# u's products over four token tiles at a time, with their operand kept in the places of two sequence tiles

## The chip, the cores and the metric

The kernel runs on one core of one Trainium2 chip. The metric is device time in microseconds (us), the median of several executions.

## What is computed

The reference mixes two branches with a gate, over S = 2048 tokens of D = 640 features:

```python
g = sigmoid((x * gate_w).sum(-1))             # one gate for each token
a = Cr @ (x @ dre.T) - Ci @ (x @ dim.T)       # Fourier mixing: sequence matrices 2048x2048, hidden 640x640
q = x @ w_q                                   # 32 heads, two halves of 128
s1, s2 = q1 @ k1.T, q2 @ k2.T                 # 16 scores a half; the best two of each, then the best two pairs
act = gelu(x @ u[e].T);  b = sum(g_e * act * v[e])   # 256 experts, two for each head
out = g * a + (1 - g) * b
```

## The kernel before, in words

Everything is float32 at full precision on TensorE: each operand is split into a high and a low part (ScalarE rounds the high part, VectorE or GpSimd subtracts to get the low one), and each product is three matmuls, high by high, high by low, low by high (`mm3`, lines 141 to 145).

**The sequence stage** is the backbone. `seq_piece(n)` (line 229) runs for n = 0 to 127. Piece n multiplies one 128x512 block of a sequence matrix (a "piece", tile `WS`, loaded as `wf`) by one split tile X[s] of x (s = n % 16, 128 tokens by 640 features, high and low): 15 matmuls of 512 columns into banks 0 to 4. Sixteen pieces make a round, with one round for each 512 columns of each of the two sequence matrices. Each piece loads piece n+5 and splits piece n+3.

**Where X lies.** Sixteen split tiles do not fit in SBUF beside the rest. In the first round (pieces 0 to 15) all sixteen lie in places X0 to X15. Tiles 0 to 8 (`AWAY = 9`) are stored to DRAM once (`put_x`, line 449, into `xd`), and their places serve others from then on. In later rounds they come back through places X6, X7 and X8 in turn (`get_x`, line 452, three pieces ahead of use). From about piece 64 they return for good.

**What is hung on the pieces.** After each piece, `follow(n)` (line 202) issues what `at(n, ...)` has put there, in the order in which it was put, so the program order of every engine and of every DMA queue is fixed when the kernel is built. Nearly all loads go through one queue, that of SyncE (SP). Each engine and the SP queue do their instructions in order, and an instruction that waits holds those behind it.

**Stage 1 (pieces 0 to 29)** also folds the query weights with the keys. The 32 loads of `wq` (640 KB each, five buffers, `load_wq` at line 353) are multiplied four at a time in `w_part` (line 358) after pieces 6, 9, ..., 27. VectorE transposes the results, and `split_w` and `make_t` prepare the score weights WU and tw. `load_u` and `split_u` bring u^T in after pieces 21 to 27. The first `store_piece` (five stores from ScalarE's queue) comes after piece 24.

**Stage 2 (pieces 30 to about 66)** computes the scores. Tokens go in eight pairs p of 128-token tiles. `split_xT(p, n)` splits x^T of a pair into `xh` and `xl` (places of their own), `sum_xT` and `split_sums_xT` make the sums for a Strassen-Winograd scheme, and `score_step(p, a)` with a = 0 to 3 runs after four pieces in a row; a piece without a step follows each odd pair. Step 0 runs six matmuls into bank 5, then `u_pair(p)` (line 720): for both halves of the experts, 15 matmuls of 256 columns into bank 7, one Gelu on ScalarE, two stores to `actd`. Then bank 5 is copied into bank 7 as the start of the next products.

**Stage 3 (pieces 66 to 127)** adds the experts' sums, built on VectorE and multiplied in groups of 48 small matmuls (line 815). **The last stage** (70 steps) applies the hidden matrices and v.

Of the kernel before, what the change touches and what calls it, by code (L numbers as in the profile page):

```python
# [17 lines left out]
P = 128  # L18
S = 2048
D = 640  # L20
# [3 lines left out]
WARM = 19  # L24
# [3 lines left out]
TC = 512  # L28
NC = S // TC
NPC = 2 * NC * NT  # L30
KD = D // P
# [7 lines left out]
KZ = KD + 1  # L39
NSTEP = 7 * KZ  # L40
AHEAD = 5
AWAY = 9
BYPASS = 4
ACCUM_END = NT * (NC + 2) - 4

# [61 lines left out]
def gated_mix_kernel(ctx: ExitStack, tc: tile.TileContext, xT, xn, dreT, dimT, wsre, wsim, wq, kT, uT, vv, gw, out):  # L107
    nc = tc.nc
# [3 lines left out]
    big = ctx.enter_context(tc.tile_pool(name="big", bufs=1))  # L112
# [9 lines left out]
    def bank(n, shape=(P, TC), dt=F32):  # L122
        return psum.tile(list(shape), dt, name=f"b{n}", tag=f"b{n}")
# [4 lines left out]
    def ps_t(shape, dt=F32):  # L128
        return bank(7, shape, dt)
# [6 lines left out]
    def split(f, h, l, eng):  # L136

        nc.scalar.activation(h, f, AF.Copy)  # L138
        eng.tensor_sub(l, f, h.bitcast(F32))  # L139

    def mm3(o, wh, wl, ah, al, first, last, more=False):

        nc.tensor.matmul(o, wh, ah, start=first, stop=False, skip_group_check=more)  # L143
        nc.tensor.matmul(o, wh, al, start=False, stop=False, skip_group_check=more)  # L144
        nc.tensor.matmul(o, wl, ah, start=False, stop=last, skip_group_check=more)  # L145
# [3 lines left out]
    actd = dram.tile([2, P, S], F32, name="actd")  # L149
# [5 lines left out]
    def run_bg(us):  # L155
        bg.run(us, share)
# [39 lines left out]
    def at(n, f, *args):  # L196
        then.setdefault(n, []).append(lambda: f(*args))
# [63 lines left out]
    p1 = p1_stack.enter_context(tc.tile_pool(name="p1", bufs=1, reuse_waits="tile"))  # L261
    pools = [p1]

    def load_x(s):
        if s < NT:
            if s % 2 == 0:
                xr[s // 2] = big.tile([P, 2, D], F32, name="xr", tag=("xf", "xh", "xl")[s // 2 % 3])
            nc.sync.dma_start(xr[s // 2][:, s % 2], xn[s])

    def split_x(s):  # L270

        if s < NT:
            X[s] = big.tile([P, 2, D], F32R, name="X", tag=f"X{s}")
# [32 lines left out]


    warm = nc.const_aps.tensor(1.0, [P, 2 * P], mybir.dt.bfloat16)
    t = ps_t([P, 2 * P])
    for n in range(WARM):  # L310
        nc.tensor.matmul(t, warm[:, :P], warm, start=True, stop=True)  # L311

    split_x(0)
    load_piece(4)
# [105 lines left out]
    def split_xT(p, n):  # L420

        if p < NP:
            if not xs:
                xs.update((t, big.tile([P, 2, KD, P], F32R, name=t, tag=t)) for t in ("xh", "xl"))
            split(xf[p][:, n], xs["xh"][:, n], xs["xl"][:, n], nc.gpsimd)

    SX = {}

# [21 lines left out]
        nc.sync.dma_start(xd[s], X[s].bitcast(F32))  # L450

    def get_x(s, tag):
        X[s] = big.tile([P, 2, D], F32R, name="X", tag=f"X{tag}")
# [76 lines left out]
    def x_part(n, k0, k1):  # L530
        return [[xs[t][:, n, k] for k in range(k0, k1)] for t in ("xh", "xl")]
# [12 lines left out]
    def score_step(p, a):  # L544


        i0, i1 = 2 * p, 2 * p + 1
        copy = lambda o, f: nc.scalar.activation(o, f, AF.Copy)  # L548
        if a == 0:
            AB["A"] = bank(5)  # L550
            products(AB["A"], (x_part(0, 0, 2), w_part2(0, 2, 0)), first=True)
            split_sums_xT(p)
            u_pair(p)
            AB["Z"] = bank(7)
            copy(AB["Z"], AB["A"])
        elif a == 1:
            products(AB["Z"], (x_part(0, 2, 4), w_part2(2, 4, 0)), (x_part(0, 4, 5), w_part2(4, 5, 0)))
            new_sc(i0)
            copy(sc_half(i0, 0), AB["Z"])
            AB["Y"] = bank(6)  # L560
            products(AB["Y"], (s_part(1), t_part(1)), first=True)
            AB["Z"] = bank(7)
            copy(AB["Z"], AB["Y"])
            load_xT(p + 1)
        elif a == 2:
            products(AB["A"], (s_part(2), t_part(2)))
            copy(sc_half(i0, 1), AB["A"])
            products(AB["Z"], (s_part(4), w_part2(2, 4, 1)), (x_part(0, 4, 5), w_part2(4, 5, 1)))
            nc.vector.tensor_add(sc_half(i0, 1), sc_half(i0, 1), AB["Z"])
            bg.credit -= 0.75  # L570
            picks(i0, scs.pop(i0))
            products(AB["A"], (s_part(3), t_part(3)))
            new_sc(i1)
            copy(sc_half(i1, 1), AB["A"])
            split_xT(p + 1, 0)
        else:
            products(AB["Y"], (x_part(1, 4, 5), w_part2(4, 5, 1)))
            nc.vector.tensor_add(sc_half(i1, 1), sc_half(i1, 1), AB["Y"])
            products(AB["A"], (x_part(1, 2, 4), t_part(4)), (x_part(1, 4, 5), w_part2(4, 5, 0)))
# [137 lines left out]
        if i % NB == NB - 1:  # L717
            bg.add(gates(i // NB))

    def u_pair(p):  # L720
        xh, xl = xs["xh"], xs["xl"]
        ps = bank(7, (P, 2, 2 * P))
        for n in range(2):
            c = slice(n * P, (n + 1) * P)
            for k in range(KD):
                mm3(ps[:, n, :], UH[:, k, c], UL[:, k, c], xh[:, :, k, :], xl[:, :, k, :], k == 0 and n == 0, k == KD - 1, True)
            run_bg(1.8)
        act = p2.tile([P, 2, 2 * P], F32, name="act")
        nc.scalar.activation(act, ps, AF.Gelu_apprx_tanh)
# [184 lines left out]
    def split_sums(k):  # L914
        if k == KD:
            f = p3.tile([P, 4 * TC], F32R, name="ts", tag="hot0")
            TS[8] = f[:, :2 * D]
            raw_free.append(f[:, 2 * D:2 * D + TC].bitcast(F32))
            raw_tags.extend((("xf", 2), ("X9", 2)))
        for n in () if k == KD else [k] + ([5 + k // 2] if k % 2 == 0 else []):  # L920
            TS[n] = big.tile([P, 2 * D], F32R, name="ts", tag=f"X{(1, 3, 4, 5, 6, 0, 2, 7)[n]}")
        t = T["t"]
        t1, t5, t3, t6 = (t[:, n * 2 * P:(n + 1) * 2 * P] for n in range(4))
        for n, f in enumerate((t1, t3, t5, t6, t[:, 8 * P:])):
            split(f, t_sum(k, n, 0), t_sum(k, n, 1), nc.gpsimd if n < 2 else nc.vector)
        bg.credit -= 1.0

    def load_v():
        T[KD] = big.tile([P, 2, D], F32, name="dt", tag="X9")
        nc.sync.dma_start(T[KD], vv.rearrange("k p d -> p k d"))  # L930

    def split_v():
# [13 lines left out]
    at(NPC + 14, store_gates, 1)  # L946


    fresh, raw_free = deque(), deque()
    raw_tags = [("X8", 2)] + [("wf", 1)] * 4 + [("X10", 2), ("wf", 1)] + [(f"X{s}", 2) for s in range(11, 16)]  # L950
    raw, sp = {}, {}

    def take(key):
# [305 lines left out]
```

## Time and profile before

| | |
|---|---|
| median of 3 runs | 754.41 us (753.17 to 755.41) |
| the profiled execution | 753.44 us, span from first to last instruction 751.7 us |
| TensorE (PE) | busy 746.7 us, 99% of the span |
| VectorE (DVE), ScalarE (ACT), GpSimd (POOL) | busy 587.4, 361.7 and 346.6 us |
| DMA | 165.89 MB, mean 221 GB/s |
| score stage in the trace | pieces 31 to 65, about 132 to 378 us |

In the profile, PE are the matmuls and PEld the weight loads, which overlap. A matmul's end is modelled and the matmuls are pipelined, so the distance between two starts, not the duration of one, is what a matmul costs in a row of them. SPq and ACTq are the DMA queues of SyncE and ScalarE. A row of the timeline shows start, time and line of an instruction (or of several alike, merged), and in brackets how long its engine stood idle before it and what ended that. "To landing" is the time from the issue of a DMA to the arrival of its last byte.

### The profile page before, as it was taken

Reading aid. Unit: us, or ns where it says so; the run is one execution under the profiler, and the core shown is the slowest. Engines: PE = TensorE matmul, PEld = TensorE weight load, DVE = VectorE, ACT = ScalarE, POOL = GpSimd, SP = SyncE. Lnnn points to the kernel's source line nnn. Section 1 sums busy time; section 2 is a strip of 40 time slices with the busy share of each in tenths; the row PEclk is TensorE's granted clock in tenths of the full one; section 3 lists DMA queues with packets and bytes.
Section 4 is the critical chain, followed back from the end, with each engine's and each line's share of the span. In section 5 each row is a group of like instructions: output and inputs, shape, how many; then the busy total and the mean of one; then the engine's idle time right before and its main releaser. Section 6 shows DMA issues by size and latency. Waiting matters only on the chain.

```text
span 751.7 us, 11366 instructions
## 1 busy us (share of the span) xinstructions
PE 746.7 (99%) x4045; PEld 610.7 (81%) x4045; DVE 587.4 (78%) x741; ACT 361.7 (48%) x660; POOL 346.6 (46%) x286
## 2 busy tenths in 40 slices
PE   9999999999999999999999999999999999999998
PEld 7777777888888888888888888888888888888887
DVE  6864088278999999998999888979999983357651
ACT  4334134534345835553734687633555653443451
POOL 5533225342424424334345445643356793487253
PEclk9999999999999999999999999999999999999999
DMA  9999999478366786663496856388766689775301
GB/s 334 378 388 356 342 381 345 132 191 278 57 174 149 184 273 164 159 167 118 121 376 210 175 146 203 116 255 291 264 225 209 218 261 335 228 233 182 112 29 71
DMA packets 84490, 165.89 MB, mean 221 GB/s; under 512 B 16081, under 2 KB 23377, under 8 KB 84177
## 3 DMA queue, kind: packets, MB, share of 16 engines
q1 hardware_dynamic: 70960, 140.89, 55.5%
q0 software_dynamic: 5472, 9.96, 8.6%
q10 hardware_dynamic: 8000, 14.31, 5.2%
q8 instruction: 32, 0.52, 0.3%
q14 instruction: 26, 0.20, 0.1%
HBM read 132.46 MB, written 31.08 MB: 218 GB/s over the span
## 4 chain that ended last, share of the span: by engine, by line
PE 96%; DMA 2%; DVE 2%; issue 0%; SPq 0%; ACT 0%
PE b L143 30%; PE b L144 30%; PE b L145 30%; PE b L239 2%; PE b L365 2%; DMA wq<-in_wq 2%; PE b L815 1%; PE b L311 1%; DVE ST L217 1%; DVE WU L139 0%; DVE tw L139 0%; DVE wp L371 0%; ACT WU L138 0%; DVE tt L397 0%; DVE tt L396 0%
## 5 line engine op out<-in xcount | busy, mean ns | idle before, releaser
L143 PE MATMUL b<-WS,X 128*128 128x512 f32 x620 | 243.5, 393 | 0.0
L144 PE MATMUL b<-WS,X 128*128 128x512 f32 x620 | 241.5, 389 | 0.0
L145 PE MATMUL b<-WS,X 128*128 128x512 f32 x620 | 241.3, 389 | 0.0
L139 POOL TENSOR_TENSOR WS<-wf,WS 128x512 fp32r<-128x512 f32 x89 | 135.9, 1532 | 162.8 <-ACT WS L138 157.9
L143 PEld LDWEIGHTS b<-WS,X 128*128 128x128 f32 x620 | 116.4, 188 | 28.0 <-issue 4.1
L145 PEld LDWEIGHTS b<-WS,X 128*128 128x128 f32 x620 | 116.4, 188 | 24.5
L144 PEld LDWEIGHTS b<-WS,X 128*128 128x128 f32 x620 | 116.4, 188 | 23.3
L138 ACT ACTIVATE WS<-wf 128x512 fp32r<-128x512 f32 x89 | 55.7, 629 | 76.9 <-PE b L145 32.1
L803 DVE TENSOR_TENSOR hot<-rows,wtab 128x1024 f16<-128x1024 f16 x64 | 62.7, 1005 | 0.7 <-PE b L815 0.6
L139 POOL TENSOR_TENSOR WS<-ra,WS 128x512 fp32r<-128x512 f32 x39 | 55.1, 1426 | 15.3 <-ACT WS L138 13.2
L139 POOL TENSOR_TENSOR xl<-xf,xh 128x640 fp32r<-128x640 f32 x16 | 28.2, 1767 | 69.3 <-ACT xh L138 62.9
L138 ACT ACTIVATE WS<-ra 128x512 fp32r<-128x512 f32 x55 | 34.5, 631 | 50.9 <-PE b L145 36.0
L548 ACT ACTIVATE sc<-b 128x512 f32<-128x512 f32 x32 | 19.2, 600 | 80.7 <-PE b L145 80.7
L191 POOL DMA_DIRECT2D WS<-in_wsre x30 | 26.4, 880 | 68.0 <-ACT WS L189 66.6
L773 ACT ACTIVATE b<-b,mask 128x128 f32<-128x128 f32 x128 | 43.0, 342 | 13.5 <-PE b L815 10.4
L139 POOL TENSOR_TENSOR WP<-ra,WP 128x512 fp32r<-128x512 f32 x18 | 26.4, 1482 | 43.2 <-ACT WP L138 43.1
L598 DVE TENSOR_TENSOR eq<-sc,mm 128x1024 f16<-128x1024 f32 x32 | 41.4, 1293 | 0.9
L605 DVE TENSOR_REDUCE tied<-eq 128x64 f32<-128x1024 f16 x32 | 39.0, 1219 | 0.9
L596 DVE TENSOR_REDUCE mm<-sc 128x64 f32<-128x1024 f32 x32 | 38.8, 1212 | 0.3
L217 DVE SCALAR_TENSOR_TENSOR ST<-ST,grow 128x512 f32<-128x512 f32 x40 | 31.4, 846 | 0.6 <-ACT ST L246 0.6
L143 PE MATMUL b<-WU,xh 128*128 128x512 f32 x80 | 31.2, 391 | 0.0
L145 PE MATMUL b<-WU,xl 128*128 128x512 f32 x80 | 31.1, 389 | 0.0
(203 smaller groups left out, 1468.8 us busy)
## 6 DMA issues: line engine op xcount, KB each, us to landing
wq<-in_wq SPq DMA_DIRECT2D x32, 640.0 KB, 7.1
X<-xd SPq DMA_DIRECT2D x30, 640.0 KB, 6.6
wf<-in_wsim SPq DMA_DIRECT2D x64, 256.0 KB, 4.8
wf<-in_wsre SPq DMA_DIRECT2D x63, 256.0 KB, 6.5
ra<-pd SPq DMA_DIRECT2D x47, 256.0 KB, 3.7
pd<-ST ACTq DMA_DIRECT2D x35, 256.0 KB, 5.2
WS<-in_wsre POOLq DMA_DIRECT2D x30, 256.0 KB, 5.3
xd<-X SPq DMA_DIRECT2D x9, 640.0 KB, 9.4
```

The lines of the kernel that those rows point to most:

```text
L138: nc.scalar.activation(h, f, AF.Copy)
L139: eng.tensor_sub(l, f, h.bitcast(F32))
L143: nc.tensor.matmul(o, wh, ah, start=first, stop=False, skip_group_check=more)
L144: nc.tensor.matmul(o, wh, al, start=False, stop=False, skip_group_check=more)
L145: nc.tensor.matmul(o, wl, ah, start=False, stop=last, skip_group_check=more)
L191: nc.gpsimd.dma_start(l, (wsre, wsim)[w][c, s], accum_op=OP.add)
L217: nc.vector.scalar_tensor_tensor(f, f, -1.0 if w else 1.0, g, op0=OP.mult, op1=OP.mult)
L596: nc.vector.tensor_reduce(m, sc, op=OP.max, axis=AX.X)
L598: nc.vector.tensor_tensor(eq, sc, m[:, :, None].to_broadcast([P, HH, E]), op=OP.is_equal)
L605: nc.vector.tensor_reduce(tied[:, s, ib, :], eq, op=OP.add, axis=AX.X)
L773: nc.scalar.activation(f[:, :, n], f[:, :, n], AF.Copy, scale=mask4[:, n:n + 1])
L803: nc.vector.tensor_tensor(o, a, b, op=op)
```

## The change

`u_pair(p)`, once for each of the eight pairs with 256 columns, becomes `u_pairs(c)`, once for two pairs with 512 columns, in step 0 of the odd pairs. For that, split x^T of two pairs must lie in SBUF together: `xh` and `xl` double to four tiles (5 KB more a partition each). They take the places of sequence tiles: X9 and X10 become one double place that holds `xh`, X11 and X12 another that holds `xl`. The places freed (the old ones of `xh` and `xl`) hold X[11] and X[12] during the score stage. ScalarE copies them there after pieces 16 and 17 and back after piece 66 (`move_x`). X[9] and X[10] are held in DRAM instead (`AWAY = 11`): they are stored after pieces 19 and 21, come back through places X6 and X7 in the second and third rounds, and are loaded for good after pieces 70 and 71. The first two loads of the hidden matrices (`load_dd`) move from pieces 70 and 72 to 71 and 74, and the buffers of the last stage are taken from the double places in another way.

The core of the diff:

```diff
-AWAY = 9
+AWAY = 11
+    def place(tag):
+        if tag in (9, 11):
+            TWIN[tag] = big.tile([P, 2, 2, D], F32R, name="X", tag=f"X{tag}")
+        if tag in (9, 10, 11, 12):
+            return TWIN[tag - (tag + 1) % 2][:, (tag + 1) % 2]
+        return big.tile([P, 2, D], F32R, name="X", tag=f"X{tag}" if isinstance(tag, int) else tag)
+
+    def move_x(s, tag):
+        old, X[s] = X[s], place(tag)
+        nc.scalar.activation(X[s], old.bitcast(F32), AF.Copy)
...
-                xs.update((t, big.tile([P, 2, KD, P], F32R, name=t, tag=t)) for t in ("xh", "xl"))
-            split(xf[p][:, n], xs["xh"][:, n], xs["xl"][:, n], nc.gpsimd)
+                xs.update((t, big.tile([P, 2, 2, KD, P], F32R, name=t, tag=tag)) for t, tag in (("xh", "X9"), ("xl", "X11")))
+            split(xf[p][:, n], xs["xh"][:, p % 2, n], xs["xl"][:, p % 2, n], nc.gpsimd)
...
-        at(6 + 2 * s, put_x, s)
+        at(6 + 2 * s if s < 9 else 1 + 2 * s, put_x, s)
     for s in range(3):
         at(2 * NT - 5 + s, get_x, s, 6 + s)
+    for s, tag in ((11, "xh"), (12, "xl")):
+        at(s + 5, move_x, s, tag)
...
             split_sums_xT(p)
-            u_pair(p)
+            act = u_pairs(p // 2) if p % 2 else lambda: None
             AB["Z"] = bank(7)
             copy(AB["Z"], AB["A"])
+            act()
...
-    def u_pair(p):
+    def u_pairs(c):
         xh, xl = xs["xh"], xs["xl"]
-        ps = bank(7, (P, 2, 2 * P))
+        def act(n, ps):
+            f = p2.tile([P, TC], F32, name="act")
+            nc.scalar.activation(f, ps, AF.Gelu_apprx_tanh)
+            nc.sync.dma_start(actd[n][:, c * TC:(c + 1) * TC], f)
         for n in range(2):
-            c = slice(n * P, (n + 1) * P)
+            e = slice(n * P, (n + 1) * P)
+            ps = bank(7 - n)
             for k in range(KD):
-                mm3(ps[:, n, :], UH[:, k, c], UL[:, k, c], xh[:, :, k, :], xl[:, :, k, :], k == 0 and n == 0, k == KD - 1, True)
-            run_bg(1.8)
-        act = p2.tile([P, 2, 2 * P], F32, name="act")
-        nc.scalar.activation(act, ps, AF.Gelu_apprx_tanh)
-        for n in range(2):
-            nc.sync.dma_start(actd[n][:, 2 * p * P:2 * (p + 1) * P], act[:, n])
+                mm3(ps, UH[:, k, e], UL[:, k, e], xh[:, :, :, k, :], xl[:, :, :, k, :], k == 0, k == KD - 1)
+                run_bg(0.68)
+            if n == 0:
+                act(n, ps)
+        return lambda: act(1, ps)
...
+    for s in (11, 12):
+        at(N1, move_x, s, s)
...
-        at(N1 + 4 + 2 * m, load_dd, m)
+        at(N1 + 5 + 3 * m, load_dd, m)
```

Where the change moves instructions, the program order shows it. On the SP queue, from the load of piece 23 on (after piece 18), before; `wq` are the query weights, `wf` sequence pieces, `xd<-X` a store of a sequence tile, `xf` the x^T of the first pair:

```order
L356 DMA wq<-in_wq 128x1280 x2
L177 DMA wf<-in_wsre 128x512
L356 DMA wq<-in_wq 128x1280 x2
L177 DMA wf<-in_wsre 128x512
L450 DMA xd<-X 128x1280
L177 DMA wf<-in_wsre 128x512
L356 DMA wq<-in_wq 128x1280 x2
L418 DMA xf<-in_xT 128x640 x2
```

and the same place with the change:

```order
L371 DMA wq<-in_wq 128x1280 x2
L177 DMA wf<-in_wsre 128x512
L465 DMA xd<-X 128x1280
L371 DMA wq<-in_wq 128x1280 x2
L177 DMA wf<-in_wsre 128x512
L465 DMA xd<-X 128x1280
L177 DMA wf<-in_wsre 128x512
L465 DMA xd<-X 128x1280
L371 DMA wq<-in_wq 128x1280 x2
L433 DMA xf<-in_xT 128x640 x2
```

The store of X[9] (640 KB) now stands ahead of the last nine loads of `wq` in this queue, and that of X[10] ahead of the last seven. On ScalarE, step 0 of the first pair before (`b_1279` is bank 5, `b_1294` and `b_1329` are bank 7):

```order
L138 ACTIVATE tw<-xf 128x256 x2
L138 ACTIVATE h<-xf 128x256 x2
L729 ACT_TABLE_LOAD
L729 ACTIVATE act<-b_1294 128x512
L548 ACTIVATE b_1329<-b_1279 128x512
```

and step 0 of the second pair with the change (`b_1479` is bank 5, `b_1495` and `b_1537` bank 7, `b_1518` bank 6):

```order
L138 ACTIVATE tw<-xf 128x256 x2
L138 ACTIVATE h<-xf 128x256 x2
L745 ACT_TABLE_LOAD
L745 ACTIVATE act<-b_1495 128x512
L565 ACTIVATE b_1537<-b_1479 128x512
L745 ACTIVATE act<-b_1518 128x512
```

An odd pair now has two Gelus around the copy, and an even pair has none: its copy follows the four splits at once.

More of the change, by code (lines that the diff above doesn't have):

```diff
@@ L262, in gated_mix_kernel @@
     pools = [p1]
+    TWIN = {}
+    def place(tag):
[7 more added lines that the diff above has]
+        nc.scalar.activation(X[s], old.bitcast(F32), AF.Copy)
     def load_x(s):
@@ L272, in split_x @@
         if s < NT:
-            X[s] = big.tile([P, 2, D], F32R, name="X", tag=f"X{s}")
+            X[s] = place(s)
             f = xr[s // 2][:, s % 2]
@@ L308, in gated_mix_kernel @@
     warm = nc.const_aps.tensor(1.0, [P, 2 * P], mybir.dt.bfloat16)
-    t = ps_t([P, 2 * P])
+    t = ps_t([P, TC])
     for n in range(WARM):
-        nc.tensor.matmul(t, warm[:, :P], warm, start=True, stop=True)
+        c = slice(0, 2 * P) if n < WARM - 1 else slice(2 * P, TC)
+        nc.tensor.matmul(t[:, c], warm[:, :P], warm, start=n < WARM - 1, stop=True, skip_group_check=n == WARM - 1)
     split_x(0)
@@ L528, in products, with x_part @@
             run_bg(0.68)
-    def x_part(n, k0, k1):
-        return [[xs[t][:, n, k] for k in range(k0, k1)] for t in ("xh", "xl")]
+    def x_part(p, n, k0, k1):
+        return [[xs[t][:, p % 2, n, k] for k in range(k0, k1)] for t in ("xh", "xl")]
     def s_part(n):
@@ L550, in score_step @@
             AB["A"] = bank(5)
-            products(AB["A"], (x_part(0, 0, 2), w_part2(0, 2, 0)), first=True)
+            products(AB["A"], (x_part(p, 0, 0, 2), w_part2(0, 2, 0)), first=True)
             split_sums_xT(p)
-            u_pair(p)
+            act = u_pairs(p // 2) if p % 2 else lambda: None
             AB["Z"] = bank(7)
             copy(AB["Z"], AB["A"])
+            act()
         elif a == 1:
-            products(AB["Z"], (x_part(0, 2, 4), w_part2(2, 4, 0)), (x_part(0, 4, 5), w_part2(4, 5, 0)))
+            products(AB["Z"], (x_part(p, 0, 2, 4), w_part2(2, 4, 0)), (x_part(p, 0, 4, 5), w_part2(4, 5, 0)))
             new_sc(i0)
@@ L567, in score_step @@
             copy(sc_half(i0, 1), AB["A"])
-            products(AB["Z"], (s_part(4), w_part2(2, 4, 1)), (x_part(0, 4, 5), w_part2(4, 5, 1)))
+            products(AB["Z"], (s_part(4), w_part2(2, 4, 1)), (x_part(p, 0, 4, 5), w_part2(4, 5, 1)))
             nc.vector.tensor_add(sc_half(i0, 1), sc_half(i0, 1), AB["Z"])
@@ L576, in score_step @@
         else:
-            products(AB["Y"], (x_part(1, 4, 5), w_part2(4, 5, 1)))
+            products(AB["Y"], (x_part(p, 1, 4, 5), w_part2(4, 5, 1)))
             nc.vector.tensor_add(sc_half(i1, 1), sc_half(i1, 1), AB["Y"])
-            products(AB["A"], (x_part(1, 2, 4), t_part(4)), (x_part(1, 4, 5), w_part2(4, 5, 0)))
+            products(AB["A"], (x_part(p, 1, 2, 4), t_part(4)), (x_part(p, 1, 4, 5), w_part2(4, 5, 0)))
             copy(sc_half(i1, 0), AB["A"])
@@ L917, in split_sums @@
             TS[8] = f[:, :2 * D]
-            raw_free.append(f[:, 2 * D:2 * D + TC].bitcast(F32))
-            raw_tags.extend((("xf", 2), ("X9", 2)))
+            raw_free.extend(LENT[0][:, a * TC:(a + 1) * TC] for a in range(2))
+            raw_tags.append(("xf", 2))
         for n in () if k == KD else [k] + ([5 + k // 2] if k % 2 == 0 else []):
@@ L928, in load_v @@
     def load_v():
-        T[KD] = big.tile([P, 2, D], F32, name="dt", tag="X9")
+        f = big.tile([P, 2, 2, D], F32, name="dt", tag="X9")
+        T[KD], f = f[:, 0], f[:, 1].rearrange("p k d -> p (k d)")
+        fresh.extend(f[:, a * TC:(a + 1) * TC] for a in range(2))
+        LENT.append(T[KD].rearrange("p k d -> p (k d)"))
         nc.sync.dma_start(T[KD], vv.rearrange("k p d -> p k d"))
@@ L946, in gated_mix_kernel @@
     at(NPC + 14, store_gates, 1)
-    fresh, raw_free = deque(), deque()
-    raw_tags = [("X8", 2)] + [("wf", 1)] * 4 + [("X10", 2), ("wf", 1)] + [(f"X{s}", 2) for s in range(11, 16)]
+    LENT, fresh, raw_free = [], deque(), deque()
+    raw_tags = [("X8", 2)] + [("wf", 1)] * 5 + [("X11", 5)] + [(f"X{s}", 2) for s in range(13, 16)]
     raw, sp = {}, {}
```

2 lines of the change are left out of this document (1 added, 1 removed).

## Prediction

> **What bounds the kernel now.** I read the page first: busy shares, then the span in forty slices.
>
> ```profile
> PE 746.7 (99%) x4045; PEld 610.7 (81%) x4045; DVE 587.4 (78%) x741; ACT 361.7 (48%) x660; POOL 346.6 (46%) x286
> PEclk9999999999999999999999999999999999999999
> DMA  9999999478366786663496856388766689775301
> ```
>
> TensorE has no idle slice and an undisturbed clock, so time is saved only by shortening its stream, and lost wherever a wait opens. The DMA row shows where one could: the first seven slices (0 to 131 us) are full. The waits of TensorE, and the rows of its timeline where they lie, say whether that already bites.
>
> ```profile
> PE b L365 <- DMA wq<-in_wq: 0.8, 2, 0.6
> 106.67 0.72 PE L365 MATMUL b<-wq,kp 128*32 128x320 f32 x8
> 107.61 0.48 PE L365 MATMUL b<-wq,kp 128*32 128x320 f32 x4 [0.22 <-DMA wq<-in_wq]
> 119.57 0.98 PE L365 MATMUL b<-wq,kp 128*32 128x320 f32 x10
> 121.17 0.48 PE L365 MATMUL b<-wq,kp 128*32 128x320 f32 x4 [0.63 <-DMA wq<-in_wq]
> ```
>
> The only two waits of TensorE for a transfer are both for query weights, at 107 and 121 us, in the full stretch. The modelled idle times (0.22 and 0.63) are short because the earlier matmuls' ends are drawn long; 24 such matmuls take 1.82 us elsewhere (0.27 for each four), so the group at 107.61 was due near 107.0 and waited 0.6 us, the one at 121.17 about 1. What matters: these loads have no slack at all.
>
> **What the change takes from TensorE.** The u products stand in the timeline between two kinds of 512-column matmuls.
>
> ```profile
> L143 PE MATMUL b<-xh,WU 128*128 128x256 f32 x80 | 22.6, 282 | 0.0
> 135.59 0.39 PE L143 MATMUL b<-WU,xh 128*128 128x512 f32 x1
> 136.95 0.28 PE L143 MATMUL b<-xh,WU 128*128 128x256 f32 x1
> 140.54 0.40 PE L143 MATMUL b<-WS,X 128*128 128x512 f32 x1
> 141.93 0.39 PE L143 MATMUL b<-WS,X 128*128 128x512 f32 x1
> ```
>
> Three groups like the first row (lines 143, 144, 145) make 240 matmuls of 256 columns. From 136.95 to 140.54 run 30 of them: 3.59 us, 0.1197 each. The six of 512 columns from 135.59 to 136.95 take 1.36 us, 0.2267 each; the six from 140.54 to 141.93 take 0.2317 each. The change replaces each two of the former by one of the latter: 120 times 0.2394 less 0.2267 is **1.5 us saved**. With 0.2317 it is 0.9; I take 1.5, since 0.2267 is measured on x^T itself. No row shows a moving operand in four runs of 128 columns (before there were two), so the lower bound is nothing saved: 0.2394 for each.
>
> The Trainium skill (TensorE: Matmul & The Clock Gate, Back-to-back issue gap) gives a matmul in a row N / 2.4 + 2.5 ns. By it the pair of 256 costs 218.3 and the 512 costs 215.8, and the saving would be 0.3 us instead of 1.5. The rows show about 13 ns over N / 2.4, not 2.5, so I stay with them.
>
> **What it adds to the SP queue in stage 1.** The two stores of X[9] and X[10] join the queue after pieces 19 and 21, at about 83 and 90 us by the rows that stand next to them there:
>
> ```profile
> 82.17 0.86 SPq L177 DMA_DIRECT2D wf<-in_wsre  x1
> 88.87 0.33 SPq L177 DMA_DIRECT2D wf<-in_wsre  x1
> 93.66 0.86 SPq L356 DMA_DIRECT2D wq<-in_wq  x2
> 98.65 5.23 SPq L356 DMA_DIRECT2D wq<-in_wq  x2
> 85.00:104.00 19.00, 19.00 (x106) 14.50 (x106) 8.54 (x16) 4.68 (x10) 6.82 (x5) 1.00 1.03 410
> 105.00:117.00 12.00, 11.78 (x73) 8.25 (x72) 10.44 (x22) 4.58 (x11) 4.24 (x3) 1.00 0.98 340
> xd<-X SPq DMA_DIRECT2D x9, 640.0 KB, 9.4
> ```
>
> In the two rows by windows the last columns are granted clock, DMA share and GB/s. From 85 to 104 us the engines are at 1.03, so there is no hole into which a store could go: the load behind it lands later by the store's whole time. A store is 640 KB, 655,360 bytes; at 410 GB/s that is 1.6 us, for two 3.2. (At 340, the rate of the stretch after it, 3.9.) The load waited for at 107.6 is the first of the two issued at 98.65 (the 28th of 32), behind both stores. So **the first wait grows by 3.2 us**. Bounds: nothing, if the engines could take more than they show; 3.9. I take 3.2, as the row of the very stretch.
>
> The second wait, at 121 us, should stay about 1 us. Its load is issued at 114.24, behind loads of u^T that themselves wait for landings, and TensorE also comes 3.2 us later; DMA is at 0.98 in the window between, so queue and TensorE move together. Bounds: minus 1.0 (it vanishes) to nothing.
>
> **What lies beside other work.** For each, the cover and the price without it:
>
> ```profile
> 131.00:378.00 247.00, 247.00 (x1202) 209.01 (x1202) 214.73 (x267) 125.56 (x201) 89.88 (x83) 1.00 0.62 166
> 376.00:398.00 22.00, 22.00 (x99) 18.22 (x98) 21.59 (x19) 7.97 (x9) 9.45 (x6) 1.00 1.00 379
> 398.00:601.00 203.00, 203.00 (x1357) 166.31 (x1356) 187.92 (x243) 115.22 (x254) 109.21 (x78) 1.00 0.69 207
> X<-xd SPq DMA_DIRECT2D x30, 640.0 KB, 6.6
> DMA to landing us min/median/max: 5.7/8.0/8.9
> ```
>
> - Four loads more of X in the score stage: DMA share 0.62, each three pieces ahead. A piece is 15 matmuls of 0.2267, 3.4 us, so three are at least 10.2 against a landing of 6.6. They make SP wait for pieces 38, 39, 54 and 55 to end, as it did for pieces 32 to 37; pieces behind it are loaded five ahead. Cost nothing.
> - Two loads for good after pieces 70 and 71, in the one other full stretch (376 to 398 us; the last row is the landing of X's loads there). Up to 8.9 us against 10.2, with the first load of the hidden matrices, of the same size, moved behind. Cost nothing; without the cover up to 2 stores' time, 3.4 us at 379 GB/s.
> - Four copies on ScalarE of 1280 columns. A split of 640 takes 0.73 us (16 of `xh` take 11.6), so each is some 1.3. ScalarE is a third busy in those stretches and has pieces split three ahead, 10.2 us. Cost nothing.
>
> ```profile
> L138 ACT ACTIVATE xh<-xf 128x640 fp32r<-128x640 f32 x16 | 11.6, 733 | 0.0
> 261.59 0.28 PE L143 MATMUL b<-xh,WU 128*128 128x256 f32 x1
> 261.61 0.71 ACT L138 ACTIVATE h<-xf 128x256 fp32r<-128x256 f32 x2
> 265.38 0.60 ACT L729 ACTIVATE act<-b 128x512 f32<-128x512 f32 x1 [3.06 <-PE b L145]
> actd<-act SPq DMA_DIRECT2D x16, 128.0 KB, 2.2
> ```
>
> - The copy of bank 5 in an even pair has less cover: 3.4 us (one piece) instead of 7.0. In the fifth pair bank 5 is complete at 261.6, ScalarE ends the four splits at 262.3, and the copy takes 0.6: done 1.3 us after, 2.1 to spare. An odd pair gains cover, 6.8 us of u and a piece.
> - The second Gelu of a pair writes the tile that the first one's store still reads, so ScalarE also waits for that store: about 0.7 for the Gelu and 2.2 to land, inside the 3.4 us of the second 15 matmuls. Behind it TensorE needs bank 6 after 24 matmuls, 5.4 us. Cost nothing; if SP is held, some tenths of a us each.
>
> **The sum**, against the profiled execution (753.44 us; its span is 751.7): minus 1.5 plus 3.2 makes 755.1. The median shown is 1.0 above that execution, so 754.41 plus 1.7: **756.1 us**.
>
> **The rivals.**
>
> 1. *The stores are hidden.* Then only the 1.5 remains: 752.9. For it: the queue has 640 KB loads in flight at 1.03, a share that could hide some reserve. Against it: 410 GB/s is the highest rate of these windows.
> 2. *The late load meets ScalarE's stores* (slower). Five stores of 256 KB leave ScalarE's queue here:
>
> ```profile
> 104.56 0.63 ACT L138 ACTIVATE WS<-wf 128x512 fp32r<-128x512 f32 x1 [0.32 <-DMA wf<-in_wsre]
> 104.64 3.93 ACTq L227 DMA_DIRECT2D pd<-ST  x5
> DMA to landing us min/median/max: 4.9/5.2/5.8
> q10 hardware_dynamic: 720, 1.31, 24.8%
> ```
>
>    The last two rows are their landing, and their bytes (queue q10) between 104 and 118 us. Today the awaited load has landed, at 107.6, before most of the 1.31 MB move. If it lands 3.2 later and the stores keep their time, they share the engines with it: another 1.31 MB at 410 GB/s, 3.2 us, on the first wait, while the second (1.0) vanishes. 754.41 - 1.5 + 6.4 - 1.0 = 758.3. It decides when the stores are issued before the piece at 104.56 is split. Against it: they stand behind that split, whose load is in the delayed queue too, so they should move along. The Trainium skill (DMA: Bandwidth & Descriptors, Queues, rings and completion order) says that each engine serves the queues that have work in turn, packet by packet; by that rule a load already waiting is not served first, which is this rival.
> 3. *Four runs save nothing*: the wait grows and the stream does not shrink: 757.6. Nothing in the rows speaks for it.
> 4. *The full stretch at 376 us gives way*: the two loads there come late by their own 3.4 us, 759.5. Against it: 8.9 against 10.2.
>
> **How the numbers follow.** Chances: the forecast 0.55 (its own range 755.0 to 757.0), the first rival 0.15, the second 0.17, the third 0.06, the fourth 0.05, anything else 0.02. The range runs from 752.6, a little under the first rival, to 758.8, above the second, and leaves out the fourth and the tails. A measurement of this kernel tells 0.3%, 2.3 us, from no change: 752.1 to 756.7. Of the forecast, 0.40 lies within, 0.14 above and 0.01 below; of the first rival 0.12 within and 0.03 below; the second and fourth lie above, the third mostly (0.05); the rest is halved between the sides. That makes faster 0.05, same 0.53, slower 0.42.
>
> **What would show it.** Right: 120 matmuls of u with starts 0.227 us apart; TensorE's wait for `wq` near 110 us at 3.8 us instead of 0.6, the later one still about 1; no wait of TensorE from 131 us on. Wrong: starts of u at 0.239; a wait that stays at 0.6 (first rival) or passes 6 us (second); waits of TensorE at bank 7 in even pairs or at pieces 73 and 74.

## The result, and the profile after

The changed kernel takes **758.71 us** (median of 14 executions, 754.03 to 760.45) against 753.77 us of the kernel before beside it: a ratio of 1.0062 (95% interval 1.0046 to 1.0077), so it is **slower, by 5 us** (0.6%). The prediction was 756.1; its range reached to 758.8 and holds the result, its own range for the forecast (755.0 to 757.0) does not. The profiled execution took 756.85 us, 3.4 more than the one before.

From the page of the changed kernel:

```profile
span 755.1 us, 11134 instructions
PE 745.5 (99%) x3925; PEld 605.1 (80%) x3925; DVE 585.4 (78%) x741; ACT 365.6 (48%) x664; POOL 348.4 (46%) x286
PEclk9999999999999999999999999999999999999999
DMA  9999999568835894882399756377875779775301
```

TensorE's waits, of the same (total, times, longest):

```profile
PE b L143 <- ACT sc L565: 2.8, 1, 2.8
PE b L380 <- DMA wq<-in_wq: 2.7, 2, 2.2
```

TensorE is busy 1.2 us less and the span is 3.4 us longer: its stream got shorter and stops took more than that back. One stop was expected, the one for `wq`. The other, on ScalarE, is new. TensorE's timeline shows both, and u between them:

```profile
93.11 1.82 PE L380 MATMUL b<-wq,kp 128*32 128x320 f32 x24
95.42 0.75 PE L380 MATMUL b<-wq,kp 128*32 128x320 f32 x8 [0.49 <-DMA wq<-in_wq]
106.54 1.82 PE L380 MATMUL b<-wq,kp 128*32 128x320 f32 x24
110.56 0.75 PE L380 MATMUL b<-wq,kp 128*32 128x320 f32 x8 [2.19 <-DMA wq<-in_wq]
121.70 2.21 PE L380 MATMUL b<-wq,kp 128*32 128x320 f32 x28
165.07 0.39 PE L143 MATMUL b<-xh,WU 128*128 128x512 f32 x1
171.87 0.39 PE L143 MATMUL b<-WS,X 128*128 128x512 f32 x1
247.12 0.39 PE L145 MATMUL b<-WU,xl 128*128 128x512 f32 x1
250.32 0.51 PE L143 MATMUL b<-tw,h 128*128 128x512 f32 x1 [2.81 <-ACT sc L565]
```

From 165.07 to 171.87 run 30 products of u: 6.80 us, 0.2267 each. In stage 1 TensorE now stops at 95 and 110 us and no longer at 121. At 247.12 it stops for 3.2 us between two starts (3.0 more than the usual 0.227): the next product goes into bank 5, which ScalarE's copy at line 565 (`sc<-b`, out of the bank) must empty first. The changed kernel's windows, to set beside those of before (the last columns are granted clock, DMA share, GB/s):

```profile
85.00:104.00 19.00, 18.51 (x104) 13.81 (x103) 7.59 (x14) 4.51 (x9) 6.29 (x5) 1.00 1.02 415
105.00:117.00 12.00, 9.80 (x65) 6.60 (x64) 8.62 (x19) 3.99 (x10) 1.60 (x2) 1.00 1.02 369
131.00:378.00 247.00, 244.19 (x1078) 201.97 (x1077) 217.22 (x275) 127.06 (x207) 88.80 (x83) 1.00 0.64 175
376.00:398.00 22.00, 22.00 (x99) 18.23 (x98) 21.55 (x20) 12.06 (x13) 8.07 (x6) 1.00 0.96 345
```

The stretch at 85 us is as full as before, so the two stores pushed the queue. The score stage carries little more DMA than before (0.64 against 0.62), yet TensorE misses 2.8 us there. The full stretch at 376 us is still free of stops.

**The chain behind the new stop**, in ScalarE's timeline of the changed kernel:

```profile
230.29 0.42 ACT L138 ACTIVATE tw<-xf 128x256 fp32r<-128x256 f32 x1 [5.50 <-DVE xf L452]
234.19 0.60 ACT L745 ACTIVATE act<-b 128x512 f32<-128x512 f32 x1
236.93 0.60 ACT L745 ACTIVATE act<-b 128x512 f32<-128x512 f32 x1 [1.53 <-DMA actd<-act]
241.96 0.63 ACT L189 ACTIVATE WS<-WS 128x512 fp32r<-128x512 f32 x1
247.94 1.90 ACT L715 ACTIVATE rows<-rt 128x384 f16<-128x384 f16 x1 [5.36 <-DMA rt<-gs]
249.35 0.91 ACT L565 ACTIVATE sc<-b 128x512 f32<-128x512 f32 x1
```

and in that of its SP queue:

```profile
234.81 3.07 SPq L746 DMA_DIRECT2D actd<-act  x2
237.97 0.38 SPq L469 DMA_DIRECT2D X<-xd  x1
238.94 2.83 SPq L710 DMA_TRANSPOSE rt<-rp  x2
241.86 1.18 SPq L710 DMA_TRANSPOSE rt<-gs  x1
```

Read them backwards. The copy at 249.35 stands behind the copy of routing rows (line 715), which stood 5.4 us until its transposing loads landed. Those were issued from 238.94 on, behind the second store of `act`; that store waited for the second Gelu (236.93), which waited 1.5 us until the first's store had landed and the one buffer of `act` was free; and the first Gelu stood behind splits that waited for VectorE until 230.29. In the kernel before the same transposes were not late. Its SP queue:

```profile
217.24 2.46 SPq L692 DMA_TRANSPOSE rt<-rp  x2
228.07 1.09 SPq L692 DMA_TRANSPOSE rt<-gs  x1
234.06 0.82 SPq L731 DMA_DIRECT2D actd<-act  x2
```

and its ScalarE:

```profile
241.09 1.93 ACT L697 ACTIVATE rows<-rt 128x384 f16<-128x384 f16 x1
```

There the first transposes stand ahead of the stores of `act`, and the last is issued 13 us before the copy of rows, which waits for nothing. In the changed kernel the background work is handed out in other portions (ten times 0.68 us in `u_pairs`, where there were two of 1.8 in each pair), so the same step comes behind the stores in the second and in the fourth of the four groups. (In the third it stood behind them before too.) In the fourth, ScalarE came for the rows 3.4 us after the last transpose was issued and found them there; in the second it came 0.7 us after, and stood.

### The profile page after: what moved, and what is told of

It reads as the page before. It is cut to its first block, busy times and chain, and to the rows that moved or that the text cites. A ratio compares the mean times of both kernels' runs of the same rounds, so it can differ in the third digit from the quotient of the medians.

```text
span 755.1 us, 11134 instructions
## 1 busy us (share of the span) xinstructions
PE 745.5 (99%) x3925; PEld 605.1 (80%) x3925; DVE 585.4 (78%) x741; ACT 365.6 (48%) x664; POOL 348.4 (46%) x286
## 4 chain that ended last, share of the span: by engine, by line
PE 88%; DVE 6%; DMA 5%; issue 0%; ACT 0%; SPq 0%; ACTq 0%; DVEq 0%
PE b L143 28%; PE b L145 27%; PE b L144 27%; DMA wq<-in_wq 3%; PE b L239 2%; PE b L380 2%; DMA xd<-X 1%; PE b L842 1%; DVE eq L616 1%; DVE tied L623 1%; DMA rt<-gs 1%; DVE mm L614 1%; DMA wf<-in_wsre 1%; DVE eq L621 1%; DVE sc L619 1%; PE b L326 1%
## 5 line engine op out<-in xcount | busy, mean ns | idle before, releaser
L139 POOL TENSOR_TENSOR WS<-wf,WS 128x512 fp32r<-128x512 f32 x89 | 139.5, 1575 | 170.9 <-ACT WS L138 163.0
L830 DVE TENSOR_TENSOR hot<-rows,wtab 128x1024 f16<-128x1024 f16 x64 | 58.4, 940 | 7.2 <-PE b L842 7.2
L139 POOL TENSOR_TENSOR xl<-xf,xh 128x640 fp32r<-128x640 f32 x16 | 26.1, 1632 | 75.6 <-ACT xh L138 75.6
L139 POOL TENSOR_TENSOR WS<-ra,WS 128x512 fp32r<-128x512 f32 x33 | 46.9, 1432 | 11.6 <-ACT WS L138 11.4
L138 ACT ACTIVATE WS<-ra 128x512 fp32r<-128x512 f32 x47 | 29.4, 631 | 42.3 <-PE b L145 30.9
L139 POOL TENSOR_TENSOR WP<-ra,WP 128x512 fp32r<-128x512 f32 x13 | 20.1, 1559 | 31.0 <-ACT WP L138 30.9
L830 DVE TENSOR_TENSOR hot<-hot,rows 128x1024 f16<-128x1024 f16 x32 | 33.0, 1032 | 0.0
L806 DVE TENSOR_REDUCE cd<-b 128x128 f32<-128x512 f32 x32 | 21.7, 682 | 12.3 <-ACT b L800 6.2
```

Of the source, the lines that this page charges most:

```text
L830: nc.vector.tensor_tensor(o, a, b, op=op)
```

## Experiments

Each difference is against the changed kernel unless the text says otherwise. The first four ran on one chip together, beside 753.69 us of the kernel before; the next four on a second chip beside 753.63; the last four on a third beside 753.54. So where a later run is set against *again*, 0.1 to 0.2 us of the difference can be the chip.

**1. again.** No edit; the changed kernel for comparison.

> The changed kernel once more, as the mark for the runs beside it. Its profile showed two new waits of TensorE: for query weights in stage 1 (about 2.0 us net) and one of 2.8 us at 247 us, where ScalarE's copy stood behind a copy of gate rows. Theory 1 (queue of stage 1) and theory 2 (SyncE's queue held by the second Gelu's store) both expect 758.7 us, 756 to 760, with both waits in the profile.

Measured 759.07 us (756.63 to 759.63), ratio 1.0063 (1.005 to 1.0077). Its profile has the same new stop, and behind it something that the first one did not show, told under "The clock" below.

**2. nostore.**

```diff
-        nc.sync.dma_start(X[s].bitcast(F32), xd[s])
+        nc.sync.dma_start(X[s].bitcast(F32), xd[s if s < 9 else s - 9])
-    for s in range(AWAY):
-        at(6 + 2 * s if s < 9 else 1 + 2 * s, put_x, s)
+    for s in range(9):
+        at(6 + 2 * s, put_x, s)
```

> Leaves out the two stores of X[9] and X[10] in stage 1; their loads bring X[0] and X[1] instead, so the output is not the reference's. Theory 1: the waits for query weights are as before the change (0.4 and 0.8 us), and the time is 2.0 us under that of the changed kernel, about 756.7; the wait in the score stage stays. The rival, that the stores are hidden and all of the loss lies in the score stage: no difference, 758.7.

Measured 756.52 us (753.91 to 758.47), 2.55 under *again*. TensorE's waits, total over `wq`: 0.6 us (before 0.8, changed 2.7). So the two stores, which this kernel leaves out, are the stage-1 loss; half of the 5 us is elsewhere.

**3. actq.**

```diff
-            nc.sync.dma_start(actd[n][:, c * TC:(c + 1) * TC], f)
+            nc.scalar.dma_start(actd[n][:, c * TC:(c + 1) * TC], f)
```

> The two stores of each Gelu's result go out from ScalarE's queue instead of SyncE's, all else as changed. Theory 2 (the second store holds SyncE's queue, the transposed loads of gate rows behind it come late, ScalarE's copy of them holds the copy that TensorE waits for): the transposed loads are issued some 2 us earlier, the wait of 2.8 us at 247 us goes or falls under 1, and the time drops by 3 us or more, to 754 to 756. Rival 3 (VectorE is late because the work of a pair now falls unevenly, 8.2 us of score products in one step and 1.4 in another): the wait stays, 758.7.

Measured **762.38 us**, 3.3 above *again*: a miss. ScalarE's timeline of this run says why:

```profile
237.54 0.60 ACT L745 ACTIVATE act<-b 128x512 f32<-128x512 f32 x1 [1.15 <-DMA actd<-act]
248.19 0.33 ACTq L746 DMA_DIRECT2D actd<-act  x1
248.56 0.63 ACT L188 ACTIVATE WS<-wf 128x512 fp32r<-128x512 f32 x1 [10.41 <-DMA X<-xd]
```

The hold had only moved. On ScalarE's queue the second store waited until 248.1 for the landing of a load of X, and all of ScalarE's work behind it stood with it for 10.4 us. So this run does not tell the theories apart.

**4. upair.** The new places, stores, moves and loads, but u as before, once for each pair with 256 columns:

```diff
-            act = u_pairs(p // 2) if p % 2 else lambda: None
+            u_pair(p)
...
-            act()
...
+    def u_pair(p):
+        xh, xl = (xs[t][:, p % 2] for t in ("xh", "xl"))
```

> u's products again for each pair with 256 columns and one Gelu a pair, but with the new places: x^T in the places of X9 to X12, X[9] and X[10] in DRAM. So the placement alone. Theories 1 and 2: no wait in the score stage, the one of stage 1 stays: 2.0 over the kernel before, about 755.8. A rival that puts the wait of the score stage on the four more loads of X in SyncE's queue: the wait is there too, 758 to 760.

Measured 756.64 us (754.74 to 757.63), ratio 1.0035 (1.0023 to 1.0048). TensorE's waits in it:

```profile
PE b L380 <- DMA wq<-in_wq: 2.6, 2, 2.1
PE b L834 <- DVE hot L822: 0.6, 1, 0.6
```

There is no stop at 247 us. So the new places cost 2.95 us, by far the most of it in stage 1, and u in groups of four tiles, which should save 1.5, costs another 2.4. The new stop belongs to `u_pairs`, not to the places.

**5. rows_later.**

```diff
-            if a > 1:
-                put_rows(a - 2, got.pop(a - 2))
+            if a > 2:
+                put_rows(a - 3, got.pop(a - 3))
-        for a in range(NB + 2):
+        for a in range(NB + 3):
```

> Each copy of routing rows by ScalarE (line 715) is moved one step later, so that it stands three transposing loads behind its own and not two; nothing else changes. Theory A: TensorE's stop of 2.8 us near 247 us in the changed kernel is ScalarE standing at this copy until its transposes land, and the copy of bank 7 that TensorE wants stands behind it. Then the stop goes (2.8 to 3.1 us, and what the slower matmuls behind it cost, 1.2 us where they show), and the time falls from 759.1 to about 755 (754 to 756). Theory B, ScalarE is late near 230 us already, because VectorE's sums of x come 2.5 us later than before: then the copy of bank 7 comes late whatever stands ahead of it, the stop shrinks to no less than 1.5 us, and the time is 757 or more.

(The last block has room for two steps' rows, so in this kernel and in *both* some of its rows are overwritten before they are copied; the amount of work is the same.) Measured 758.35 us, not the 755 of theory A. TensorE's waits in it:

```profile
PE b L380 <- DMA wq<-in_wq: 2.5, 2, 1.9
PE b L144 <- DMA WS<-in_wsim: 0.9, 2, 0.5
PE b L144 <- POOL WS L139: 0.9, 1, 0.9
PE b L143 <- DMA X<-xd: 0.6, 1, 0.6
```

The stop at 247 us is gone without a rest, which is against theory B: ScalarE's splits still waited 5.50 us for VectorE near 230 us, and TensorE did not notice. (The bank that TensorE waited for is bank 5, not bank 7 as the expectation says.) But others came, near 321, 421, 445 and 508 us. The one at 421 us stands in most runs with `u_pairs`, as the next part tells; that the edit made the rest, by holding the three `rt` buffers longer, was not tried.

**6. gelu_later.**

```diff
             copy(AB["Z"], AB["A"])
-            act()
+            AB["act"] = act
...
             copy(sc_half(i0, 0), AB["Z"])
+            AB["act"]()
             AB["Y"] = bank(6)
```

> The second Gelu of a four-tile group, and its store, come at the end of the score step after (ahead of the next use of bank 6), and not at once behind the first Gelu, whose store must land before the one buffer of act is free. Theory A1, SP is held at the second store until the second Gelu has run (from 233.3 to 235.7 us), and the transposing loads behind it start 2 to 2.4 us late: with that hold gone the copy of rows is released 2 us sooner or more, the stop near 247 us shrinks from 2.8 to under 0.8 us, and the time falls to 755 to 756.5. Theory A2, the hold is small beside the order itself: the transposes and the copy that reads them stand some 14 matmuls (3 us) apart in the program while a transposing load takes 6 to 8 us to land, so the stop stays at 2 us or more and the time at 758 or more.

Measured **760.85 us**, against both theories. TensorE's waits separate two things:

```profile
PE b L143 <- ACT act L746: 4.7, 4, 1.2
PE b L380 <- DMA wq<-in_wq: 3.1, 2, 2.0
```

The stop behind the copy of rows is gone (the transposes landed at 245.7 us, and ScalarE came for them at 246.2). That speaks for A1 but does not show it: the transposes were issued at 238.9 us as in the first profile of the changed kernel, while all work around them ran 2.7 us later in this run (the first Gelu at 236.92), and ScalarE itself came later still. My edit made four stops of its own: just behind the Gelu TensorE takes bank 6 again and now waits for it in every group.

**7. stores_late.**

```diff
-        at(6 + 2 * s if s < 9 else 1 + 2 * s, put_x, s)
+        at((25, 26)[s - 7] if s in (7, 8) else 6 + 2 * s if s < 9 else 1 + 2 * s, put_x, s)
```

> The stores of X[7] and X[8] to DRAM move from behind pieces 20 and 22 to behind pieces 25 and 26, after the last loads of wq: so stage 1 stores as many bytes ahead of these as the kernel before. Theory 1, the two added stores alone delay wq: the wait at 108 us falls back to about 0.5 us and stage 1 gives back 2.0 us, or 3.6 where the matmuls behind that wait ran slow: 756.5 (755 to 757.5). Rival, what delays wq is where X[9] to X[12] lie (one slot for two) and not the bytes: the wait stays above 1.5 us and the time at 758 or more.

Measured 757.18 us (755.47 to 761.15), 1.9 under *again*; its ratio of 1.005 (1.003 to 1.007) overlaps that of *again*, so the waits are the better evidence. The one at 108 us is gone, those at 95 and 121 us are 0.7 and 1.1, together 1.8 us for `wq`. Bytes moved behind the loads of `wq` delay them less, though not all comes back.

**8. both**, edits 5 and 7.

> The later copies of rows and the later two stores together, on the changed kernel. If the two stops are all that the change costs, what stays is the gain of 512-wide products of u, 1.5 to 1.6 us: 753.7 - 1.5 = 752.2 (751.5 to 753). If a cost elsewhere is left (four more loads of X, the four moves by ScalarE, the slower matmuls), the time is 753.5 or more.

Measured 756.21 us (754.15 to 757.83): a cost elsewhere is left. In the profile it is 1.8 us for `wq`, a load of X at 320 us (1.6 us), as in *rows_later*, and 0.9 us each at 420 and 507 us.

**9. gelu_first.** The cause taken at its root: the first Gelu stands ahead of the splits of x's sums.

```diff
-            split_sums_xT(p)
-            act = u_pairs(p // 2) if p % 2 else lambda: None
+            act = u_pairs(p // 2) if p % 2 else split_sums_xT(p)
...
             if n == 0:
                 act(n, ps)
+                split_sums_xT(2 * c + 1)
```

> On the changed kernel, ScalarE runs the first Gelu of a four-tile group ahead of the splits of x's sums and not behind them; the order of SP's transfers is the same, each piece of work is the same. In the run of the changed kernel beside it bank 7 was complete at 228.5 us, but the Gelu ran at 232.3, behind splits that waited for VectorE. Theory A1 (SP is held at the second store until the second Gelu, which waits for the first's store to land): first Gelu and store 2.3 us sooner, second Gelu and store 2.3 us sooner, transposing loads from 234.8 and not 237.05 us, and the stop near 247 us falls from 2.8 to under 0.8 us: 759.1 goes to 755 to 756.5, with the slower matmuls behind that stop gone too. Theory A2 (the order alone, transposes and their reader 3 us apart while they take 6 to 8 us to land): the stop stays at 2 us or more and the time at 758 or more.

Measured **753.91 us** (752.38 to 756.65, 12 executions), ratio to the kernel before 1.0005 (0.9994 to 1.0016): 5.2 us under *again*, more than A1 gave. The stop itself is 3.1 of it: the eight executions with a clock of 0.999 or more have a median of 753.54 us, the four such of the changed kernel and *again* together 756.69. The rest is slow stretches (see "The clock" below), of which only four executions here had one. Part of that is luck: *upair* has the same loads and stores in stage 1, no stop at 247 us either, and a stretch in four of six. ScalarE of *gelu_first* in the same stretch:

```profile
228.13 0.60 ACT L745 ACTIVATE act<-b 128x512 f32<-128x512 f32 x1 [4.45 <-PE b L145]
231.53 0.60 ACT L745 ACTIVATE act<-b 128x512 f32<-128x512 f32 x1 [1.00 <-PE b L145]
242.47 1.95 ACT L715 ACTIVATE rows<-rt 128x384 f16<-128x384 f16 x1 [2.30 <-DMA rt<-gs]
```

its SP queue:

```profile
228.76 3.72 SPq L746 DMA_DIRECT2D actd<-act  x2
233.54 2.75 SPq L710 DMA_TRANSPOSE rt<-rp  x2
```

and the whole stretch by windows:

```profile
226.00:260.00 34.00, 34.00 (x152) 27.98 (x151) 31.92 (x39) 21.84 (x33) 10.67 (x11) 1.00 0.69 170
```

Both Gelus now wait for TensorE alone. The transposes start 5.4 us after the first half of u is complete (228.1 to 233.5), where the changed kernel took 8.6 (230.3 to 238.9). The copy of rows stands 2.3 us and not 5.4, and TensorE is busy for all of the 34 us: those 2.3 are covered. The order on SP is the same as in the changed kernel. So theory A2 (the order alone) falls: the order made room for the stop, and the late Gelus filled it.

**10. first_and_late**, edits 7 and 9.

> The first Gelu ahead of the splits and the stores of X[7] and X[8] behind pieces 25 and 26, together, on the changed kernel. Both stops were made smaller by one of these alone, so the time should be 753.7 - 1.5 (512-wide products of u) + 0.8 (what the later stores left of stage 1) + 0.4 (rest of the stop at 247 us) + 1.0 (a stop at 422 us that most runs of the changed kernel's order had) = 754.4 (753 to 755.5), a tie with the kernel before. Below 753 the two stops were dearer than their lengths; above 756 there is a third cost that no run has shown.

Measured 753.39 us (751.77 to 757.05), ratio 0.9992 (0.9977 to 1.0007). This is the best form of the change, and a tie with the kernel before.

**11. stores_alone**, on the kernel before:

```diff
+    spare = dram.tile([2, P, 2, D], F32, name="spare")
...
+    for s in (9, 10):
+        at(1 + 2 * s, lambda s: nc.sync.dma_start(spare[s - 9], X[s].bitcast(F32)), s)
```

> The kernel before with two stores of 640 KB more, of X[9] and X[10] to spare DRAM, behind pieces 19 and 21; nothing reads them and nothing else is changed. Theory 1 (the bytes alone delay wq): stage 1 grows by 1.5 to 2.0 us in stops, and by up to 1.6 us where matmuls run slow behind a stop of over 2 us: 755.4 to 757. Rival (not the bytes but the new places of X[9] to X[12], the moves or later loads): within 0.5 us of the kernel before, 753.2 to 754.2.

Measured 756.65 us (756.32 to 758.23), ratio 1.0039 (1.0026 to 1.0051): two stores that nobody reads cost as much as all of *upair* (756.64). So it is the bytes of the two stores, and the moves, later loads and double places cost nothing that can be seen.

**12. pauses**, on the kernel before:

```diff
-            copy(AB["Z"], AB["A"])
+            for _ in range(1 + {0: 6, 2: 7, 4: 8, 6: 10}.get(p, 0)):
+                copy(AB["Z"], AB["A"])
```

> The kernel before with TensorE made to stop four times: in the score steps of pairs 0, 2, 4 and 6, ScalarE repeats its 0.58 us copy from bank 5 to bank 7, on which TensorE waits with 2.02 us to spare, 6, 7, 8 and 10 times more; so stops of about 1.6, 2.2, 2.9 and 4.1 us near 144, 208, 272 and 338 us. If the clock that the throttle grants falls behind a stop of over about 2.1 us (8 matmuls at 427 and not 227 ns, as behind 8 of the 10 such stops in the runs so far, and behind none of the shorter), the longer three cost 1.6 us more each: 753.7 + 10.8 + 4.8 = 769.3, at least 767. If a stop costs its own length and no more, 764.5.

Measured 767.01 us (765.7 to 768.59), the median of four, between the two. It is read under "The clock".

**The clock.** Behind the stop at 245 us in *again*, by windows (the second number is TensorE's busy time, the third from the end the granted clock):

```profile
245.30:248.70 3.40, 0.73 (x4) 0.39 (x3) 1.64 (x2) 2.33 (x2) 0.00 (x0) 1.00 0.70 168
248.71:252.11 3.40, 3.40 (x10) 2.63 (x9) 3.30 (x4) 1.22 (x3) 0.00 (x0) 0.50 0.98 370
```

and in TensorE's timeline of *stores_alone*:

```profile
109.99 1.29 PE L366 MATMUL b<-wq,kp 128*32 128x320 f32 x8 [2.55 <-DMA wq<-in_wq]
111.80 0.63 PE L144 MATMUL b<-WS,X 128*128 128x512 f32 x1
112.23 0.63 PE L145 MATMUL b<-WS,X 128*128 128x512 f32 x1
```

For 3.4 us (in the profile of *stores_alone* for 6.8) the granted clock is one half and 512-column matmuls start 0.427 us apart, not 0.227: in 3.4 us some 8 of them, 1.6 us lost. Over all profiled runs, by the distance between two starts: of 25 gaps from 1.0 to 2.2 us none was followed by such a stretch; of twelve from 2.3 to 3.2 us eight were (not the two of the first profile, nor the middle two of *pauses*); both gaps over 4 us were. One such stretch lowers the mean clock of an execution by some 0.002 (half of 3.4 of 755 us), so that number counts them: 0.999 in the profile of the changed kernel, which has none, 0.998 in that of *again* with one, 0.995 in that of *actq* with two.

What decides is where a stop falls. In each of the 14 profiles the clock changes only at whole multiples of 3.41 us after its first rise to full speed, and that rise comes at a different time in each, from 3.5 to 6.7 us. Cut into windows at these points, the profiles divide without exception: after a window at full clock in which TensorE was busy for 1.48 us or less, the next ran at half clock (ten cases while matmuls still followed); after 1.59 us or more, it did not. The 3.0 us stop at 247 us in the first profile was cut in two by such a point, and each window kept enough work:

```profile
245.45:248.85 3.40, 2.06 (x10) 1.36 (x8) 2.86 (x3) 0.91 (x1) 0.00 (x0) 1.00 1.04 91
248.86:252.26 3.40, 1.94 (x8) 1.61 (x9) 1.91 (x2) 1.64 (x3) 0.00 (x0) 1.00 0.77 235
```

Of the 14 executions of the changed kernel three had 0.999 or 1.000 and took 754.03 to 756.85 us, three 0.997 or 0.998 (757.72 to 758.47), and eight 0.995 or 0.996 (757.95 to 760.45). So the profile shown here is one of the lucky ones, and the median holds one to two slow stretches more. In *pauses* the four stops add up to 11.2 us, which makes 764.7 without stretches; its two executions at 0.998 took 765.70 and 766.02 us, the two at 0.996 took 767.99 and 768.59, as one and two stretches would have it.

The Trainium skill (TensorE: Matmul & The Clock Gate, "What's actually happening") says that the clock is halved after an idle window of about 3.4 us that runs freely. The half clock, the length of the window and its free phase agree with these traces; that the window must be idle does not: 1.48 us of work in it was still too little.

## Why the prediction was right in its range and wrong in its reasons

- **What bounds the kernel**: right. TensorE's stream got shorter by what the wider matmuls saved, and every stop went straight into the time. Two readings were off: by the distances of starts the two waits for `wq` were 0.4 and 0.8 us, not 0.6 and about 1; and the landing of 6.6 us, set there against the loads of X in the score stage, is the median over the whole run.
- **u's products, 1.5 us saved**: right. 30 matmuls in 6.80 us, where two pairs took 7.18: 0.38 a group, 1.5 in four. By the 2.5 ns over N / 2.4 of the Trainium skill (TensorE: Matmul & The Clock Gate, Back-to-back issue gap) it would have been 0.3; this kernel does not show that.
- **The two stores, 3.2 us on the first wait, the second unchanged**: the mechanism was right (the stores push the loads of `wq` back), its terms mis-sized. Two stores alone give 756.65 (*stores_alone*), and without them 2.55 us come back (*nostore*). But in the first profile the first wait grew by 2.0 us only, a new one of 0.7 came at 95 us, and the second, forecast to stay, vanished (0.8). Over the seven profiled runs with this stage 1 the waits for `wq` are 1.2 to 3.1 us against 0.8. The rest of the 2.5 to 3 us is the slow stretch that often follows, a term that the sum did not have: *upair* took 754.74 and 755.54 us in the executions without one, 756.37 to 757.63 in those with one.
- **"The second Gelu ... waits for that store ... Cost nothing; if SP is held, some tenths of a us each"**: this is the step that failed. The cover named, the 3.4 us of the second 15 matmuls, was enough for TensorE's bank 6, but the first Gelu was itself 3.8 us late behind splits that wait for VectorE (in *again*, bank 7 complete at 228.5, Gelu at 232.3), so SP was held (in the first profile to 237.6 us), and behind it stood transposes that ScalarE came for at 242.6. I named what waits behind the Gelu on TensorE, and not what waits behind the store on SP: 3.0 us of stop and mostly a slow stretch with it.
- **No wait of TensorE from 131 us on**: wrong for that reason, and for one more: eight of the ten profiled runs with `u_pairs` (not the first, nor *gelu_later*) have another stop of about 1 us at 417 to 427 us, for an adding load of `WS`; the four runs without `u_pairs` have none. In *again*, on GpSimd and TensorE:

```profile
416.20 5.34 POOL L139 TENSOR_TENSOR WS<-wf,WS 128x512 fp32r<-128x512 f32 x1 [1.53 <-ACT WS L138]
421.49 0.87 POOL L191 DMA_DIRECT2D WS<-in_wsim  x1
423.15 0.50 PE L144 MATMUL b<-WS,X 128*128 128x512 f32 x1 [0.74 <-DMA WS<-in_wsim]
```

GpSimd issues that load itself, behind a subtraction that took 5.34 us here. All ten runs with `u_pairs` have such a subtraction, at 411 to 421 us; in the four others none near there takes over 2.4. That it is what delays the load is read from the order of these rows; no edit removed it.

- **Four loads more, two loads for good, four copies, bank 5 in even pairs: cost nothing**: right. TensorE did not stop at any of them, and *upair* costs no more than the two stores.
- **The rivals**: hidden stores (752.9) fell with *stores_alone*. The second rival's 758.3 is near the result, but by no part of its mechanism: the wait at 108 us did not pass 3 us in any run. Since the top of the range was set by that rival, it is luck that the range holds the result, by 0.1 us. The full stretch at 376 us held.

The sum now, on 753.8: minus 1.5 for u, plus some 1.5 of stops in stage 1, 3.0 at 247 us, 0.8 (eight tenths of 1.0) near 420 us, and 1.4 slow stretches of 1.6: 759.8, one above the 758.7 measured, as near as single profiles allow.

## What to carry to other kernels

When one instruction becomes dependent on a later event, follow every queue that its consumer stands in, not just the engine: here a Gelu was off the path, its store held SP, and SP's next loads were on ScalarE's path and so on TensorE's. A program order made by a background pump shifts with any change of its portions, so look at the whole order for pairs of load and reader that have come close. And count a stop of TensorE of over 2.3 us as its length plus up to 1.6 us, as it falls into the clock's windows.

## What the runs showed of the hardware that was not expected

- A gap of 2.36 us in TensorE's stream can bring 3.4 us at half the clock, and the same program has them or not from one execution to the next, since the windows of 3.41 us lie differently each time. That is most of the spread of the changed kernel (6.4 us over 14 executions, against 2.5 us before, where of 51 executions beside the experiments two had a clock under 0.999).
- A store issued from ScalarE's queue can hold ScalarE for the landing of a load that another queue issued: 10.4 us in *actq*.
- A subtraction of GpSimd took 5.34 us instead of 1.3 to 1.7, at 416.7 us in the changed kernel. It ended at 422.1 us, 1.2 after a row of VectorE's 16-bit products (`hot<-rows`) that had run beside it without a break; in *gelu_first* the row ended at 415.4 us and the subtraction at 416.6. It looks as if it could not go on until the row was over, but no run tried that.
